# One load per head for V, wo ahead of the values, and a four-group closing in a cached decode-attention kernel

## The chip, the cores and the metric

The kernel runs on one core of a Trainium2 chip. TensorE multiplies, VectorE and ScalarE do elementwise work and reductions, GpSimd does small elementwise work, and SyncE (SP) issues the transfers; 16 DMA engines carry them out. The metric is the device time of one execution, in microseconds. Before the change it is 220.58 us, the median of three runs (220.52 to 221.18).

## The reference

One decode step of two batch rows, `x` of 2 x 512. Everything is float32.

```python
W = 4096                                     # the last 4096 of 32768 cached positions
q = (x @ wq)                                 # 32 query heads of 128; 8 KV heads, 4 queries share one
scores = einsum("bhqd,bhkd->bhqk", q, k) * 128 ** -0.5
p = softmax(scores)
a = einsum("bhqk,bhkd->bhqd", p, v).reshape(B, 1, 32 * 128) @ wo     # 4096 x 512
h = einsum("bsd,df->bsf", x, w1) + b1        # 512 x 1792
b = einsum("bsf,fd->bsd", h * tanh(softplus(h)), w2)                 # 1792 x 512
g = sigmoid((x * gate_w).sum(-1))
return g * a + (1 - g) * b
```

K and V in the window are 33.5 MB each; wq and wo 8.4 MB each; w1 and w2 3.7 MB each. Each of these bytes is used once.

## The kernel before, in words

The work is a loop of eight rounds, one for each KV head, on every engine. Buffers are single: `kslot` holds one head's K (128 x 8192) and the next head's slice of wq (128 x 2048); `vslot` holds V (128 x 8192, named `vs`), a slice of w2 (`w2s`, 128 x 1024) and a slice of wo (`wos`, 128 x 2048). w1 is resident in `w1s`. The last slice of wo has its own place, `wol`.

A round goes so. When K has landed, TensorE makes the scores `sc` (line 233: 16 products in four column groups of 32), while VectorE makes the next head's queries (line 325) and then copies them into `qz` (line 288). VectorE takes the maximum `mx` (line 329), TensorE transposes it into `mb` (line 239), VectorE makes the bias (line 333), ScalarE the exponentials (line 214), TensorE their sums `lp` (line 240), VectorE transposes the probabilities to `pT` (line 335). TensorE then multiplies them with V into `o` (line 244: 16 products of 128x512, again four column groups; products 0 to 7 use the first half of V). Of `o` (128 x 512) only one 128-column block in each row group is wanted. VectorE picks it with four masked multiply-adds into `osc` (lines 342 and 344; `mkr` is mask, gate and one over the sum). TensorE folds the row groups with one product into `ol` (line 257, tile `small`), and VectorE copies it to `wst2` (line 347). The MLP's hidden units go the same way once a round: VectorE multiplies w1 with x and sums (lines 336, 292, 298), GpSimd and ScalarE apply Mish, and the result goes to `hst`. With two products of w2 (line 253) and four of wo (line 260) the round adds both into the PSUM tile `acc`. These use the attention output and hidden units of the round before, so the slices of w2 and wo that come with V belong to the head before.

SP issues all transfers in program order, and each waits for its buffer to be free: K of the next head for `qz` (VectorE has used both the scores' operands and wq), the first half of V for `sV` (TensorE is through products 0 to 7 of `o`), the rest with w2 and wo for `sP` (the round's last product of wo is done). In the last round K comes in three pieces, V in three (`va`, `v7b`, `v7c`), then w2 (`w26`), wo of head 6 (`wo6`) and wo of head 7 in three pieces (`wo7a`, `wo7b`, `wo7c`).

After the loop ScalarE copies `acc` to `accs` (line 218), and TensorE folds it and multiplies the last slice of wo in the function `last`: each call makes two products of 256 columns in two column groups, with two row halves of `fin` for two sets of calls. ScalarE copies one half (line 220), VectorE adds the other (line 351), and SP stores `res`.

Of the kernel before, what the change touches and what calls it, by code (L numbers as in the profile page):

```python
# [36 lines left out]
def decode_kernel(nc, xg, wq0, w1, kw, k7a, k7b, k7c, va, vb0, vb, v7b, v7c, w26, wo6, wo7a, wo7b, wo7c, out):  # L37
# [78 lines left out]
    for i in range(HKV):  # L116
# [7 lines left out]
        if i:  # L124
            SP.wait_ge(sem["sV"], i)
        SP.dma_start(vs[:, : 2 * h], va[i]).then_inc(sem["ld_v"], L)
        if i:
            SP.wait_ge(sem["sP"], i)
        if i == 0:
            SP.dma_start(vs[:, 2 * h :], vb0).then_inc(sem["ld_vb"], L)  # L130
            SP.dma_start(w1s[:, : PAIRS * W1P], w1).then_inc(sem["ld_w"], L)
        elif i < PAIRS:
            SP.dma_start(vslot[:, 2 * h : CHUNK + 2 * D + WQH], vb[i - 1]).then_inc(sem["ld_vb"], L)
        else:
            SP.dma_start(vs[:, 2 * h : 3 * h], v7b).then_inc(sem["ld_vb"], L)
# [76 lines left out]
    with A.Fori(1, HKV + 1, 1) as r:
# [3 lines left out]
        A.activation(pq, pq, AF.Exp).then_inc(sem["hq"], 1)  # L216
# [1 line left out]
    A.copy(accs, acc).then_inc(sem["accs"], 1)
# [1 line left out]
    A.copy(fs, fin[64:, :256]).then_inc(sem["fs"], 1)  # L220


    key_rhs = same[:, :16].rearrange("p (b n h) -> p b n h", b=B, n=NH)[:, :, 0, :]
    with T.Fori(1, HKV + 1, 1) as r:
# [27 lines left out]
        for j in range(2):
            i = T.matmul(acc[Q * j : Q * j + Q, :], hst[:, j * Q : j * Q + Q], w2s[:, j * D : j * D + D],  # L253
                         start=False, stop=False, skip_group_check=True)
# [2 lines left out]
        after(T.matmul(ol, osel, key_rhs, start=True, stop=True), "osel").then_inc(sem["sE"], 1)  # L257
        T.wait_ge(sem["ld_o"], loads)
        for j in range(REP):
            i = T.matmul(acc[Q * j : Q * j + Q, :], wst[:, j * Q : j * Q + Q], wos[:, j * D : j * D + D],  # L260
                         start=False, stop=False, skip_group_check=True)
        i.then_inc(sem["sP"], 1)

    def last(s, lhs, rhs, wait=None, **kw):
        for u in range(2):
# [1 line left out]
            i = T.matmul(fin[a : a + Q, :256], lhs, rhs[:, u * 256 : u * 256 + 256], skip_group_check=True, **kw)  # L267
# [137 lines left out]
```

## Time and profile before

| | us |
|---|---|
| median of three runs | 220.58 |
| profiled execution, its own time | 220.1 |
| its span, first to last instruction | 218.8 |
| TensorE busy | 118.8 (54%) |
| VectorE busy | 126.2 (58%) |
| ScalarE busy | 10.3 (5%) |
| GpSimd busy | 26.2 (12%) |
| DMA queue q1, share of 16 engines' span | 97.8% |

Busy shares are averages over the span. "PE" is TensorE's matmuls, "PEld" its weight loads, "DVE" VectorE, "ACT" ScalarE, "POOL" GpSimd, "SPq" the queue of SP. A float32 product appears as two matmul records and two weight loads. "PEclk" is the clock that TensorE was granted: 1.00 is full, 0.50 half. A row of a timeline can merge several like instructions that follow each other; its count stands behind the x, and the square bracket tells how long the engine had been idle before, and what ended that.

### The profile page before, as it was taken

How to read it: one execution, taken by the hardware profiler on the slowest of the kernel's cores; microseconds unless marked ns; L12 is line 12 of the kernel's file. 1: busy time of each engine (PE TensorE's matmuls, PEld its weight loads, DVE VectorE, ACT ScalarE, POOL GpSimd, SP SyncE). 2: the span in 40 equal slices, each digit the busy share in tenths (PEclk: the TensorE clock that was granted, in tenths of full speed). 3: DMA queues.
4: the chain of work that ended last, by engine and by line, in shares of the span. 5: the costliest groups of instructions: out<-in, count | busy, mean ns of one | idle time of the engine just before them, and what ended most of it. 6: DMA issues, size and time to landing. Idle time of an engine off the chain costs nothing.

```text
span 218.8 us, 1985 instructions
## 1 busy us (share of the span) xinstructions
PE 118.8 (54%) x668; PEld 31.1 (14%) x668; DVE 126.2 (58%) x268; ACT 10.3 (5%) x28; POOL 26.2 (12%) x118
## 2 busy tenths in 40 slices
PE   0006386058463477807547195924648175984775
PEld 0002021012110112202111022101112022120211
DVE  2897913919743468507673177714693075967850
ACT  2000010000100001000100001000100001000101
POOL 8200000220021000310012000210002100050030
PEclk9999958757969675875988757695996958599599
DMA  8898999989999999989999899999999899999993
GB/s 310 367 479 371 453 446 407 479 377 429 451 434 442 401 437 455 464 374 452 435 407 479 377 429 446 439 442 401 437 455 464 374 446 440 392 412 442 412 410 118
DMA packets 4926, 91.29 MB, mean 417 GB/s; under 512 B 552, under 2 KB 572, under 8 KB 1084
## 3 DMA queue, kind: packets, MB, share of 16 engines
q1 hardware_dynamic: 4924, 91.26, 97.8%
q8 instruction: 1, 0.02, 0.0%
q14 instruction: 1, 0.01, 0.0%
HBM read 91.26 MB, written 0.00 MB: 417 GB/s over the span
## 4 chain that ended last, share of the span: by engine, by line
DMA 73%; PE 15%; DVE 8%; SPq 2%; issue 1%; DVEq 0%
DMA vslot<-in_vb 51%; DMA w1s<-in_w 15%; PE o L244 9%; DMA wol<-in_wo7a 8%; PE acc L260 4%; DVE osc L344 3%; PE small L257 1%; DVE osc L342 1%; DVE junk L292 1%; DVE hxt L298 1%; PE fin L267 1%; SPq L113 0%; DVE w1c L336 0%; DVE xs L300 0%; SPq L137 0%
## 5 line engine op out<-in xcount | busy, mean ns | idle before, releaser
L233 PE MATMUL sc<-kslot,zeros 128*32 128x512 f32 x256 | 42.7, 823 | 51.5 <-DMA kslot<-in_kw 50.2
L325 DVE CUSTOM_DVE_ANT_0 junk<-kslot,xs 128x512 f32<-128x512 f32 x64 | 39.8, 686 | 37.4 <-DMA kslot<-in_kw 36.4
L244 PE MATMUL o<-vslot,pT 128*32 128x512 f32 x256 | 48.2, 897 | 12.8 <-DMA vslot<-in_vb 10.1
L233 PEld LDWEIGHTS sc<-kslot,zeros 128*32 128x32 f32 x256 | 10.7, 145 | 83.2 <-issue 80.4
L187 POOL TENSOR_TENSOR hb<-hxt,zeros 128x4 f32<-128x4 f32 x8 | 1.7, 216 | 147.0 <-DVE hxt L298 147.0
L292 DVE TENSOR_TENSOR junk<-w1c,xs 128x2048 f32<-128x2048 f32 x8 | 18.3, 2293 | 0.3
L298 DVE TENSOR_REDUCE hxt<-junk 128x4 f32<-128x2048 f32 x8 | 18.3, 2286 | 0.3
L244 PEld LDWEIGHTS o<-vslot,pT 128*32 128x32 f32 x256 | 9.2, 147 | 42.4 <-issue 19.1
L342 DVE TENSOR_SCALAR osc<-o,mkr 128x128 f32<-128x128 f32 x8 | 2.8, 351 | 15.1 <-PE o L244 15.1
L214 ACT ACTIVATE prob<-sc,bias 128x512 f32<-128x512 f32 x8 | 5.5, 687 | 118.7 <-DVE bias L333 118.7
L257 PE MATMUL small<-same,osc 128*128 128x8 f32 x16 | 3.3, 280 | 12.7 <-DVE osc L344 12.7
L240 PE MATMUL small<-lsum,same 128*128 128x1 f32 x16 | 4.1, 324 | 10.5 <-ACT prob L214 10.5
L260 PE MATMUL acc<-vslot,zeros 128*32 128x512 f32 x64 | 9.4, 662 | 0.6 <-DMA vslot<-in_wo 0.6
L335 DVE STREAM_TRANSPOSE pT<-prob 128x512 f32<-128x512 f32 x8 | 5.7, 712 | 6.8 <-ACT prob L214 6.8
L336 DVE COPY w1c<-w1s 128x1024 f32 x8 | 5.2, 656 | 7.5 <-DMA w1s<-in_w 7.5
L344 DVE SCALAR_TENSOR_TENSOR osc<-o,mkr,osc 128x128 f32<-128x128 f32 x24 | 8.4, 351 | 0.9
L253 PE MATMUL acc<-vslot,zeros 128*32 128x512 f32 x32 | 8.6, 616 | 0.3 <-DMA vslot<-in_w 0.3
L329 DVE TENSOR_REDUCE mx<-sc 128x1 f32<-128x512 f32 x8 | 5.5, 691 | 5.6 <-PE sc L233 5.6
L239 PE MATMUL mb<-ident,mx 128*128 128x128 f32 x8 | 2.6, 322 | 9.1 <-DVE mx L329 9.1
L257 PEld LDWEIGHTS small<-same,osc 128*128 128x128 f32 x16 | 2.6, 203 | 20.2 <-DVE osc L344 20.2
L325 DVE DVE_READ_ACCUMULATOR2_ANT q<- 128x1 f32 x64 | 5.2, 81 | 0.0
L240 PEld LDWEIGHTS small<-lsum,same 128*128 128x128 f32 x16 | 3.4, 265 | 12.0 <-ACT prob L214 12.0
(63 smaller groups left out, 64.8 us busy)
## 6 DMA issues: line engine op xcount, KB each, us to landing
kslot<-in_kw SPq DMA_DIRECT2D x7, 5120.0 KB, 19.3
vslot<-in_vb SPq DMA_DIRECT2D x6, 3584.0 KB, 18.9
vslot<-in_va SPq DMA_DIRECT2D x8, 2048.0 KB, 19.9
w1s<-in_w SPq DMA_DIRECT2D x1, 3584.0 KB, 32.7
vslot<-in_vb SPq DMA_DIRECT2D x1, 2048.0 KB, 24.6
kslot<-in_k7a SPq DMA_DIRECT2D x1, 2048.0 KB, 11.1
vslot<-in_wq SPq DMA_DIRECT2D x1, 1031.0 KB, 5.2
kslot<-in_k7b SPq DMA_DIRECT2D x1, 1024.0 KB, 13.2
```

The costliest lines, as they stand in the source:

```text
L214: A.activation(prob, sc, AF.Exp, bias=bias, scale=SCALE, accum_out=lsum).then_inc(sem["ex"], 1)
L233: i = T.matmul(sc[Q * j : Q * j + Q, :], qz[:, m * Q : m * Q + Q], ks[:, (m * NJ + j) * 512 : (m * NJ + j + 1) * 512], start=(m == 0), sto ...
L240: after(T.matmul(lp, same, lsum, start=True, stop=True), "ex").then_inc(sem["sC"], 1)
L244: i = T.matmul(o[Q * j : Q * j + Q, :], pT[:, c * Q : c * Q + Q], vs[:, c * 512 : c * 512 + 512], start=(c < NJ), stop=(c >= NC - NJ))
L253: i = T.matmul(acc[Q * j : Q * j + Q, :], hst[:, j * Q : j * Q + Q], w2s[:, j * D : j * D + D], start=False, stop=False, skip_group_check= ...
L257: after(T.matmul(ol, osel, key_rhs, start=True, stop=True), "osel").then_inc(sem["sE"], 1)
L260: i = T.matmul(acc[Q * j : Q * j + Q, :], wst[:, j * Q : j * Q + Q], wos[:, j * D : j * D + D], start=False, stop=False, skip_group_check= ...
L292: return V.tensor_tensor(out.rearrange("p (b c d) -> p b c d", b=B, c=n), lhs.rearrange("p (c d) -> p c d", c=n)[:, None, :, :].to_broadca ...
L298: return V.tensor_reduce(out, junk[:, : n * D].rearrange("p (c d) -> p c d", d=D), axis=AX.X, op=ALU.add)
L325: i = V.tensor_tensor_reduce(out=junk[:, (h * B + b) * D : (h * B + b) * D + D], in0=wqs[:, h * D : h * D + D], in1=xb[b], op0=ALU.mult, o ...
L335: after(V.transpose(pT, prob), "ex").then_inc(sem["pT"], 1)
L344: after(V.scalar_tensor_tensor(osc[:, m * DH : m * DH + DH], o[:, m * DH : m * DH + DH], mkr[:, m : m + 1], osc[:, m * DH - DH : m * DH], ...
```

## The change

It is one edit of many parts.

- **V in one load.** For the heads 1 to 6, one transfer (`vw`) brings wo, V and w2; head 0 brings V in one. It is issued when `sP` comes. `sV` is gone. In the last round the first piece (`v7a`) holds wo of head 6 and the first half of V, so that `wo6` is no transfer of its own, and lies ahead of `v7b`, `v7c` and `w26` in the queue. The bias b1 moves to the front of `vslot`, padded to 16 columns.
- **wo ahead of the values.** On TensorE the four products of wo stand ahead of those of `o`, and `sP` is raised by the w2 products.
- **Output copied by ScalarE in halves.** ScalarE copies `o` to `osb` in two pieces of 256 columns. VectorE's four masked steps are gone.
- **Masked in small products.** `kmr` (128 x 32: mask, gate, one over the sum and row-group key) is made by VectorE right after the transpose of the probabilities, from the constant `m4gk` that GpSimd makes once. Four small products of `osb` with slices of `kmr` accumulate into `ol`, behind the raising of `sP`.
- **Closing in four column groups.** `last` makes four products of 128 columns, one in each column group; there are five calls, fold first. VectorE copies `fin` to `res` (128 x 128) alone.
- **Loop at a block boundary.** An alignment instruction stands ahead of TensorE's loop.

```diff
-        if i:
-            SP.wait_ge(sem["sV"], i)
-        SP.dma_start(vs[:, : 2 * h], va[i]).then_inc(sem["ld_v"], L)
-        if i:
-            SP.wait_ge(sem["sP"], i)
         if i == 0:
-            SP.dma_start(vs[:, 2 * h :], vb0).then_inc(sem["ld_vb"], L)
+            SP.dma_start(vs, v0).then_inc(sem["ld_v"], L)
             SP.dma_start(w1s[:, : PAIRS * W1P], w1).then_inc(sem["ld_w"], L)
-        elif i < PAIRS:
-            SP.dma_start(vslot[:, 2 * h : CHUNK + 2 * D + WQH], vb[i - 1]).then_inc(sem["ld_vb"], L)
+            continue
+        SP.wait_ge(sem["sP"], i)
+        if i < PAIRS:
+            SP.dma_start(row, vw[i - 1]).then_inc(sem["ld_v"], L)
         else:
+            SP.dma_start(row[:, : WQH + 2 * h], v7a).then_inc(sem["ld_v"], L)
             SP.dma_start(vs[:, 2 * h : 3 * h], v7b).then_inc(sem["ld_vb"], L)
             SP.dma_start(vs[:, 3 * h :], v7c).then_inc(sem["ld_vc"], L)
             SP.dma_start(w2s, w26).then_inc(sem["ld_h"], L)
-    SP.dma_start(wos, wo6).then_inc(sem["ld_o"], L)
...
+        A.wait_ge(sem["sD"], r)
+        for m in range(2):
+            A.copy(osb[:, m * 2 * DH : m * 2 * DH + 2 * DH], o[:, m * 2 * DH : m * 2 * DH + 2 * DH]).then_inc(sem[f"os{m + 1}"], 1)
     A.wait_ge(sem["sP"], HKV)
     A.copy(accs, acc).then_inc(sem["accs"], 1)
-    A.wait_ge(sem["pe"], 1)
-    A.copy(fs, fin[64:, :256]).then_inc(sem["fs"], 1)
...
+    T.addr_align(256, offset=0, max_nops=0)
     with T.Fori(1, HKV + 1, 1) as r:
...
         T.wait_ge(sem["ld_v"], loads)
+        for j in range(REP):
+            i = T.matmul(acc[Q * j : Q * j + Q, :], wst[:, j * Q : j * Q + Q], wos[:, j * D : j * D + D],
+                         start=False, stop=False, skip_group_check=True)
+            if j == 0:
+                after(i, "hs")
         for c in range(NC):
             j = c % NJ
             i = T.matmul(o[Q * j : Q * j + Q, :], pT[:, c * Q : c * Q + Q], vs[:, c * 512 : c * 512 + 512],
                          start=(c < NJ), stop=(c >= NC - NJ))
             if j == 0 and c != NJ:
                 after(i, ("pT", "", "ld_vb", "ld_vc")[c // NJ])
-            if c == NC // 2 - 1:
-                i.then_inc(sem["sV"], 1)
         i.then_inc(sem["sD"], 1)
         T.wait_ge(sem["ld_h"], loads)
         for j in range(2):
             i = T.matmul(acc[Q * j : Q * j + Q, :], hst[:, j * Q : j * Q + Q], w2s[:, j * D : j * D + D],
                          start=False, stop=False, skip_group_check=True)
             if j == 0:
-                after(i, "hs")
-        after(T.matmul(ol, osel, key_rhs, start=True, stop=True), "osel").then_inc(sem["sE"], 1)
-        T.wait_ge(sem["ld_o"], loads)
-        for j in range(REP):
-            i = T.matmul(acc[Q * j : Q * j + Q, :], wst[:, j * Q : j * Q + Q], wos[:, j * D : j * D + D],
-                         start=False, stop=False, skip_group_check=True)
+                after(i, "kmr")
         i.then_inc(sem["sP"], 1)
-
-    def last(s, lhs, rhs, wait=None, **kw):
-        for u in range(2):
-            a = Q * (2 * s + u)
-            i = T.matmul(fin[a : a + Q, :256], lhs, rhs[:, u * 256 : u * 256 + 256], skip_group_check=True, **kw)
-            if wait is not None and u == 0:
+        for m in range(BN):
+            i = T.matmul(ol, osb[:, m * DH : m * DH + DH], kmr[:, m * B * REP : (m + 1) * B * REP],
+                         start=(m == 0), stop=(m == BN - 1))
+            if m % 2 == 0:
+                after(i, f"os{m // 2 + 1}")
+        i.then_inc(sem["sE"], 1)
+
+    def last(lhs, rhs, wait, **kw):
+        for u in range(NJ):
+            i = T.matmul(fin[Q * u : Q * u + Q, :P], lhs, rhs[:, u * P : u * P + P], skip_group_check=True, **kw)
+            if u == 0:
                 i.wait_op(*wait, "sem-ge")
         return i
 
-    def wo(j):
-        return wst2[:, j * Q : j * Q + Q], wol[:, j * D : j * D + D]
-
+    last(fold, accs, (sem["accs"], 1), start=True, stop=False)
     T.wait_ge(sem["wst"], HKV)
-    last(0, *wo(0), (sem["ld_w0"], L), start=True, stop=False)
-    last(1, *wo(1), start=True, stop=False)
-    last(0, fold, accs, (sem["accs"], 1), start=False, stop=False)
-    last(1, *wo(2), (sem["ld_w1"], L), start=False, stop=True).then_inc(sem["pe"], 1)
-    last(0, *wo(3), (sem["ld_w2"], L), start=False, stop=True).then_inc(sem["pe"], 1)
+    for j, (n, value) in enumerate((("ld_w0", L), ("wst", HKV), ("ld_w1", L), ("ld_w2", L))):
+        i = last(wst2[:, j * Q : j * Q + Q], wol[:, j * D : j * D + D], (sem[n], value), start=False, stop=(j == REP - 1))
+    i.then_inc(sem["pe"], 1)
...
+        after(V.reciprocal(rcp, lp), "sC").then_inc(sem["rcp"], 1)
+        after(V.tensor_scalar_mul(kmr, m4gk, rcp), "rcp").then_inc(sem["kmr"], 1)
         at(V.tensor_copy(w1c, w1s[:, bass.ds((r - 1) * W1P, W1P)]), "ld_w", 2 * L).then_inc(sem["w1c"], 1)
         after(products(junk[:, : 2 * B * D], w1c, 2), "w1c").then_inc(sem["w1p"], 1)
         after(sums(hxt, 2 * B), "w1p").then_inc(sem["hx"], 1)
-        after(V.reciprocal(rcp, lp), "sC").then_inc(sem["rcp"], 1)
-        after(V.tensor_scalar_mul(mkr, m4g, rcp), "rcp").then_inc(sem["mkr"], 1)
-        V.wait_ge(sem["sD"], r)
-        after(V.tensor_scalar_mul(osc[:, :DH], o[:, :DH], mkr[:, 0:1]), "mkr").then_inc(sem["os1"], 1)
-        for m in range(1, BN):
-            after(V.scalar_tensor_tensor(osc[:, m * DH : m * DH + DH], o[:, m * DH : m * DH + DH], mkr[:, m : m + 1],
-                                         osc[:, m * DH - DH : m * DH], op0=ALU.mult, op1=ALU.add),
-                  f"os{m}").then_inc(sem["osel" if m == BN - 1 else f"os{m + 1}"], 1)
         after(V.tensor_copy(wst2v, ol.rearrange("p (b h) -> p h b", b=B)), "sE").then_inc(sem["wst"], 1)
         after(V.reciprocal(mr, md), "hd").then_inc(sem["hr"], 1)
     V.addr_align(128, offset=0, max_nops=0)
-    V.wait_ge(sem["fs"], 1)
-    at(V.tensor_tensor(res, fin[:64, :256], fs, op=ALU.add), "pe", 2).then_inc(sem["res"], 1)
+    at(V.tensor_copy(res, fin[:, :P]), "pe", 1).then_inc(sem["res"], 1)
...
-        "va": v[:, :, : 2 * h],
-        "vb0": v[0, :, 2 * h :],
-        "vb": np.concatenate([v[1:PAIRS, :, 2 * h :], w2[:NP], wo[:NP]], axis=2),
+        "v0": v[0],
+        "vw": np.concatenate([wo[: NP], v[1:PAIRS], w2[:NP]], axis=2),
+        "v7a": np.concatenate([wo[NP], v[PAIRS, :, : 2 * h]], axis=1),
         "v7b": v[PAIRS, :, 2 * h : 3 * h], "v7c": v[PAIRS, :, 3 * h :],
-        "w26": w2[NP], "wo6": wo[NP],
+        "w26": w2[NP],
```

On SP, from the load of head 6's K to the end, the transfers stood in this order before (`kw` is K with wq; `va`, `vb`, `v7b`, `v7c` are pieces of V; `w` is the last w2, `wo` the slice of head 6):

```order
L120 DMA kslot<-in_kw 128x10240
L126 DMA vslot<-in_va 128x4096
L133 DMA vslot<-in_vb 128x7168
L123 DMA kslot<-in_k7a 128x4096
L123 DMA kslot<-in_k7b 128x2048
L123 DMA kslot<-in_k7c 128x2048
L126 DMA vslot<-in_va 128x4096
L135 DMA vslot<-in_v7b 128x2048
L136 DMA vslot<-in_v7c 128x2048
L137 DMA vslot<-in_w 128x1024
L138 DMA vslot<-in_wo 128x2048
```

And now:

```order
L119 DMA kslot<-in_kw 128x10240
L129 DMA vslot<-in_vw 128x11264
L122 DMA kslot<-in_k7a 128x4096
L122 DMA kslot<-in_k7b 128x2048
L122 DMA kslot<-in_k7c 128x2048
L131 DMA vslot<-in_v7a 128x6144
L132 DMA vslot<-in_v7b 128x2048
L133 DMA vslot<-in_v7c 128x2048
L134 DMA vslot<-in_w 128x1024
```

Two rows became one for each of the heads 1 to 6, and the row of `wo` went up into `v7a`; the three pieces of `wo7` follow in both.

On TensorE, in the loop and behind it (- before, + now; `mb` and `small` are the maximum's transpose and the sums, `o` the values, `acc` the products of w2 and wo, `fin` the closing):

```order
 L239 MATMUL mb<-ident,mx 128x128
 L240 MATMUL small<-lsum,same 128x1
-L244 MATMUL o<-vslot,pT 32x512 x16
-L253 MATMUL acc<-vslot,zeros 32x512 x2
-L257 MATMUL small<-same,osc 128x8
-L260 MATMUL acc<-vslot,zeros 32x512 x4
+L243 MATMUL acc<-vslot,zeros 32x512 x4
+L249 MATMUL o<-vslot,pT 32x512 x16
+L256 MATMUL acc<-vslot,zeros 32x512 x2
+L262 MATMUL small<-kmr,osb 128x8 x4
```

The four products of wo moved from the round's end to a place ahead of the values, and the fold into `ol` (tile `small`) is four products at the end of the round.

More of the change, by code (lines that the diff above doesn't have):

```diff
@@ L34, with decode_kernel @@
 NP = PAIRS - 1
-def decode_kernel(nc, xg, wq0, w1, kw, k7a, k7b, k7c, va, vb0, vb, v7b, v7c, w26, wo6, wo7a, wo7b, wo7c, out):
+def decode_kernel(nc, xg, wq0, w1, kw, k7a, k7b, k7c, v0, vw, v7a, v7b, v7c, w26, wo7a, wo7b, wo7c, out):
     T, V, A, G, SP = nc.tensor, nc.vector, nc.scalar, nc.gpsimd, nc.sync
@@ L49, in decode_kernel @@
     w1c = sb("w1c", W1P)
-    vslot = sb("vslot", CHUNK + 2 * D + WQH + 2 * HKV)
-    vs, w2s, wos = vslot[:, :CHUNK], vslot[:, CHUNK : CHUNK + 2 * D], vslot[:, CHUNK + 2 * D : CHUNK + 2 * D + WQH]
-    b1 = vslot[:, CHUNK + 2 * D + WQH : CHUNK + 2 * D + WQH + FC]
+    vslot = sb("vslot", Q // B + WQH + CHUNK + 2 * D)
+    b1, row = vslot[:, :FC], vslot[:, Q // B :]
+    wos, vs, w2s = row[:, :WQH], row[:, WQH : WQH + CHUNK], row[:, WQH + CHUNK :]
     wol = sb("wol", REP * D)
@@ L80, in decode_kernel @@
     rcp = sb("rcp", 1)
-    mkr = sb("mkr", BN)
-    osc = sb("osc", BN * DH)
-    osel = osc[:, (BN - 1) * DH :]
+    m4gk = sb("m4gk", BN * B * REP)
+    kmr = sb("kmr", BN * B * REP)
+    osb = sb("osb", BN * DH)
     junk = sb("junk", B * REP * D)
@@ L93, in decode_kernel @@
     accs = sb("accs", D)
-    fs = sb("fs", 256, 64)
-    res = sb("res", 256, 64)
+    res = sb("res", P)
     acc = ps("acc", D)
@@ L104, in decode_kernel @@
     ol = small[:, 8:16]
-    names = ("ld_x ld_q ld_k ld_kb ld_kc ld_v ld_vb ld_vc ld_w ld_h ld_o ld_w0 ld_w1 ld_w2 c_id c_m c_z c_xb c_eg c_g c_mg "
-             "gx g0 g1 g2 g3 g4 g5 hs vx q8 rcp os1 os2 os3 qz mx sA sB bias ex pT sC osel sD sP sE sV wst pq mkr w1c w1p hx hq hd hr accs pe fs res st").split()
+    names = ("ld_x ld_q ld_k ld_kb ld_kc ld_v ld_vb ld_vc ld_w ld_h ld_w0 ld_w1 ld_w2 c_id c_m c_z c_xb c_eg c_g c_mg "
+             "gx g0 g1 g2 g3 g4 g5 hs vx q8 rcp os1 os2 qz mx sA sB bias ex pT sC sD sP sE wst pq kmr w1c w1p hx hq hd hr accs pe res st").split()
     sem = {n: nc.alloc_semaphore(n) for n in names}
-    SP.dma_start(vslot[:, CHUNK + 2 * D : CHUNK + 2 * D + WQH + FC], wq0).then_inc(sem["ld_q"], L)
+    SP.dma_start(vslot[:, : Q // B + WQH], wq0).then_inc(sem["ld_q"], L)
     SP.wait_ge(sem["c_xb"], 2)
@@ L174, in decode_kernel @@
     G.wait_ge(sem["c_g"], 1)
-    G.tensor_tensor(m4g.rearrange("p (b n) -> p b n", n=NH), m2[:, :BN].rearrange("p (b n) -> p b n", n=NH),
-                    g[:, :, None].to_broadcast([P, B, NH]), op=ALU.mult)
-    G.tensor_scalar(omg, g, -1.0, 1.0, op0=ALU.mult, op1=ALU.add).then_inc(sem["c_mg"], 1)
+    done(G.tensor_tensor(m4g.rearrange("p (b n) -> p b n", n=NH), m2[:, :BN].rearrange("p (b n) -> p b n", n=NH),
+                    g[:, :, None].to_broadcast([P, B, NH]), op=ALU.mult))
+    G.tensor_scalar(omg, g, -1.0, 1.0, op0=ALU.mult, op1=ALU.add)
+    G.tensor_tensor(m4gk.rearrange("p (m b h) -> p m b h", b=B, h=REP),
+                    same[:, :16].rearrange("p (b n h) -> p b n h", b=B, n=NH)[:, :, 0, :][:, None].to_broadcast([P, BN, B, REP]),
+                    m4g[:, :, None, None].to_broadcast([P, BN, B, REP]), op=ALU.mult).then_inc(sem["c_mg"], 1)
     G.wait_ge(sem["c_mg"], 1)
@@ L205, in decode_kernel @@
                         omg[:, None, :].to_broadcast([P, 2, B]), op=ALU.mult).then_inc(sem["hs"], 1)
-    for n in ("ld_kb", "ld_kc", "ld_vc", "ld_o", "ld_h"):
+    for n in ("ld_kb", "ld_kc", "ld_vb", "ld_vc", "ld_h"):
         A.sem_inc(sem[n], AHEAD)
@@ L349, in decode_kernel @@
     V.addr_align(128, offset=0, max_nops=0)
-    V.wait_ge(sem["fs"], 1)
-    at(V.tensor_tensor(res, fin[:64, :256], fs, op=ALU.add), "pe", 2).then_inc(sem["res"], 1)
+    at(V.tensor_copy(res, fin[:, :P]), "pe", 1).then_inc(sem["res"], 1)
     SP.wait_ge(sem["res"], 1)
-    SP.dma_start(out, res[:: Q // B, :]).then_inc(sem["st"], L)
+    SP.dma_start(out.rearrange("b u x -> u b x"), res[:: Q // B, :]).then_inc(sem["st"], L)
     SP.wait_ge(sem["hs"], HKV + 1)
@@ L399 @@
             for n, t in arrays.items()]
[L400 removed]
+    args.append(nc.dram_tensor("out_0", (B, NJ, P), F32, kind="ExternalOutput").ap())
     decode_kernel(nc, *args)
     r = run_bass_kernel_spmd(nc, [{f"in_{n}": t for n, t in arrays.items()}], core_ids=[0])
[L403 to L404 removed]
+    y = r.results[0]["out_0"]
+    return c(y).reshape(B, 1, D)
```

6 lines of the change are left out of this document (1 added, 5 removed).

## The prediction

> **What bounds the kernel now.** I began with the page's DMA part and the table of busy time by stretches, because a kernel that uses each byte once may have nothing left but its transfers.
>
> ```profile
> span 218.8 us, 1985 instructions
> ...
> q1 hardware_dynamic: 4924, 91.26, 97.8%
> q8 instruction: 1, 0.02, 0.0%
> ```
>
> ```profile
> 2.00:50.00 48.00, 16.98 (x89) 4.71 (x93) 29.07 (x47) 1.54 (x5) 7.17 (x28) 0.84 0.99 425
> ...
> 150.00:200.00 50.00, 32.69 (x194) 8.57 (x194) 32.67 (x79) 1.97 (x6) 5.90 (x24) 0.79 1.01 430
> 200.00:213.00 13.00, 8.84 (x49) 2.39 (x41) 8.99 (x18) 0.99 (x3) 1.71 (x9) 0.74 1.00 414
> 213.00:216.00 3.00, 2.60 (x26) 0.75 (x28) 0.00 (x0) 0.79 (x2) 0.67 (x4) 1.00 0.69 255
> 216.00:218.80 2.80, 0.41 (x4) 0.00 (x0) 0.42 (x1) 0.16 (x1) 0.00 (x0) 1.00 0.01 1
> ```
>
> The columns behind the length are the busy time of PE, PEld, DVE, ACT and POOL, then the granted clock, the DMA share and GB/s. The DMA share is 0.99 to 1.01 from 2 us to 213 us: the 16 engines never run dry, and no compute inside the loop sets the time, though the chain of waits passes through it. Only three things can move the end: how long the transfers take, whether the queue runs dry, and what follows the last landings. The span ends 218.8 us and the execution counts 220.1, so 1.3 us lie outside it.
>
> So I read the end next, from the timeline.
>
> ```profile
> 204.49 5.95 PE L244 MATMUL o<-vslot,pT 128*32 128x512 f32 x32 [0.90 <-DMA vslot<-in_va]
> ...
> 209.38 0.16 PEld L244 LDWEIGHTS o<-vslot,pT 128*32 128x32 f32 x8 [1.27 <-DMA vslot<-in_v7c]
> ...
> 209.99 0.21 ACT L216 ACTIVATE pq<-pq 128x8 f32<-128x8 f32 x1 [7.04 <-POOL pq L191]
> ...
> 210.73 1.05 PE L253 MATMUL acc<-vslot,zeros 128*32 128x512 f32 x4 [0.29 <-DMA vslot<-in_w]
> ...
> 212.15 0.30 PEld L257 LDWEIGHTS small<-same,osc 128*128 128x128 f32 x2 [1.27 <-DVE osc L344]
> 212.15 0.39 PE L257 MATMUL small<-same,osc 128*128 128x8 f32 x2 [0.36 <-DVE osc L344]
> 212.57 0.17 DVE L347 COPY wst<-small 128x8 f32<-128x8 f32 x1 [0.48 <-PE small L257]
> ...
> 213.15 0.16 PEld L260 LDWEIGHTS acc<-vslot,zeros 128*32 128x32 f32 x8 [0.70 <-DMA vslot<-in_wo]
> ...
> 214.28 0.59 ACT L218 COPY accs<-acc 128x512 f32<-128x512 f32 x1 [4.08 <-PE acc L260]
> ...
> 214.43 0.16 PEld L267 LDWEIGHTS fin<-wol,wst 128*32 128x32 f32 x8 [1.12 <-DMA wol<-in_wo7a]
> ...
> 215.36 1.05 PE L267 MATMUL fin<-wol,wst 128*32 128x256 f32 x6
> 215.78 0.14 PEld L267 LDWEIGHTS fin<-wol,wst 128*32 128x32 f32 x4 [0.52 <-DMA wol<-in_wo7c]
> 215.79 0.37 ACT L220 COPY fs<-fin 64x256 f32<-64x256 f32 x1 [0.93 <-PE fin L267]
> 216.46 0.42 DVE L351 TENSOR_TENSOR res<-fin,fs 64x256 f32<-64x256 f32 x1 [3.63 <-PE fin L267]
> ```
>
> Each product that starts on a landing tells when that landing came: the first half of V 204.49, v7c 209.38, w26 about 210.7, wo6 213.15, wo7a 214.43, wo7c 215.78. Behind the last one stand 0.63 us of products (to 216.41), 0.42 us of VectorE and the store. Everything between v7c and wo7c had 6.4 us of transfers to hide under.
>
> **The transfers.** Eight transfers vanish: one for each of heads 0 to 6, and wo6. The bytes stay. The price of a transfer's boundary comes from the same rows: 1,024 KB took 2.45 us (wo6, 210.70 to 213.15); 512 KB took 1.32 (w26) and 1.28 (wo7a); twice 256 KB took 1.35 (wo7b and c). Two halves cost 0.15 more than the whole, two quarters 0.03 to 0.07 more than a half. I take 0.08 for each, nearer the smaller ends because the rows give 0.01 us and handovers blur the rest: 8 x 0.08 = 0.64 us, with 0.2 and 1.2 as ends. That moves every landing near the end forward.
>
> [...]
>
> **Does the queue run dry?** V is now reloaded in one piece after the whole round, where its first half used to go out early. The shortest cover is head 7's K.
>
> ```profile
> 189.63 2.91 PE L244 MATMUL o<-vslot,pT 128*32 128x512 f32 x16 [0.32 <-DMA vslot<-in_vb]
> ...
> 195.70 0.33 SPq L135 DMA_DIRECT2D vslot<-in_v7b  x1
> ...
> 199.49 0.16 PEld L233 LDWEIGHTS sc<-kslot,zeros 128*32 128x32 f32 x8 [2.19 <-DMA kslot<-in_k7c]
> ```
>
> From head 6's V landing (189.63) to K's end (199.49) lie 9.9 us. TensorE then has six steps of four products: wo, four of values, and w2 (two products, but two passes all the same). A step's length depends on the granted clock.
>
> ```profile
> 186.53 0.20 PEld L244 LDWEIGHTS o<-vslot,pT 128*32 128x32 f32 x4 [0.66 <-issue]
> ...
> 187.38 0.20 PEld L244 LDWEIGHTS o<-vslot,pT 128*32 128x32 f32 x4 [0.66 <-issue]
> ...
> 195.46 0.13 PEld L233 LDWEIGHTS sc<-kslot,zeros 128*32 128x32 f32 x4 [0.30 <-issue]
> 195.89 0.13 PEld L233 LDWEIGHTS sc<-kslot,zeros 128*32 128x32 f32 x4 [0.30 <-issue]
> ```
>
> ```profile
> 48.60:51.73 3.13, 3.06 (x16) 0.92 (x20) 3.13 (x11) 0.00 (x0) 0.00 (x0) 0.50 1.01 429
> ...
> 184.85:191.68 6.83, 6.28 (x30) 1.69 (x34) 6.17 (x6) 0.02 (x1) 0.47 (x3) 0.50 0.93 398
> ...
> 201.92:208.74 6.82, 4.83 (x23) 1.63 (x26) 5.91 (x6) 0.78 (x2) 0.00 (x0) 0.50 0.97 404
> 208.74:218.70 9.96, 6.14 (x50) 1.37 (x42) 2.56 (x10) 1.16 (x3) 2.38 (x12) 1.00 0.65 256
> ```
>
> Four loads are two products: 0.85 us at clock 0.50, 0.43 at 1.00. A step is 1.70 cold and 0.86 warm. A burst after a pause starts cold and warms after 3.1 us (48.60 row), 4.25 (204.49 to 208.74), or as much as 6.8 (184.85 row). Call that x; n steps take x + (n - x/1.70) x 0.86. [...]
>
> Six steps take 7.3 us at x = 4.25 and 8.5 at 6.8. The issue takes 0.33, and a store took 1.1 us from its issue's end to landing, which bounds the delay to first data:
>
> ```profile
> SPq L357 <- DMA out<-res: 1.1, 1, 1.1
> ```
>
> That makes 8.7 to 9.95 us against 9.9. So I cost the late reload at nothing; in earlier rounds K is 5,120 KB instead of 4,096 KB and the cover longer still. On SP only the next K waits behind it, and that needs the scores of a K not yet landed.
>
> **The end, worked out.** wo now precedes v7a's values, so this landing comes at 204.49 + 2.45 - 0.64 = 206.30. TensorE's five steps (wo, sixteen values) end, with the same burst's x = 4.25, at 4.25 + 2.5 x 0.86 = 6.40, so 212.70. v7c (209.38 + 2.45 - 0.64 = 211.19) and w26 (212.51) have landed by then. w2: 0.86, to 213.56; `sP` rises and ScalarE's `accs` (0.59) hides under what follows. ScalarE's two copies of `o` were started at 212.7; at 0.37 each (64x256 row; 128x512 took 0.59) they are done by 213.6, and their place behind the exponential of `pq` costs nothing, because that ran at 209.99. Four small products: two loads in 0.30 each and a drain of 0.09: 1.29, to 214.85. Their copy on VectorE with handovers (212.54 to 212.77): 0.23, to 215.08. The fold ran meanwhile. A closing call of four 128-column products is a quarter of a warm step, 0.215: three of them to 215.72. The last: 0.215 plus the drain seen before (0.63 less two passes of 0.215) 0.20, to 216.14. Before it was 216.41: 0.27 saved.
>
> Then VectorE copies 128x128 from PSUM. This exact form is not in the trace; it lies between 0.17 (128x8) and 0.35 (`osc`, same size, multiply):
>
> ```profile
> L342 DVE TENSOR_SCALAR osc<-o,mkr 128x128 f32<-128x128 f32 x8 | 2.8, 351 | 15.1 <-PE o L244 15.1
> ```
>
> I take 0.30 for 0.42: 0.12 saved. ScalarE's half (0.37) overlapped TensorE and frees nothing. The sum is 0.27 + 0.12 = 0.39: 220.1 becomes 219.7. The median of the runs is 0.48 above the profiled execution, so **220.2 us**.
>
> The point is that the end changes its owner: 0.64 us of earlier landings and a shorter close are mostly eaten by TensorE's longer path after v7a, since 1 MB that used to lie behind the values now lies ahead of them. The last landing, 215.14, would allow 215.14 + 0.42 = 215.56.
>
> At nothing I cost: the four removed VectorE steps, about 1.5 us a round, since the reload has the cover above; `kmr` ahead of w1 (it needs two small operations beside products on TensorE); `m4gk`, one GpSimd operation before the first round, under head 0's loads; and the alignment, executed while TensorE waits for the first K. That the branch back cost a code load each round is not seen: queue q8 shows one packet in the span.
>
> The ends: with x = 3.1 the values end at 212.13 and w26's landing decides: 212.51 + 0.86 + 1.29 + 0.23 + 0.64 + 0.42 = 215.95, 220.0 in all. With x = 6.8 they end at 213.96 and the products at 217.40: 0.99 - 0.12 = 0.87 later, 221.45. The ends of the transfers' price shift this by +0.4 and -0.6.
>
> **Rivals.** *A, faster: the close hides again.* If the small products overlap (their weight loads can run under the w2 products) and warm clock comes early, the last landing decides: 215.56, so 0.85 + 0.12 = 0.97 saved, 219.6; with 1.2 us from the transfers 219.1. For it: weight loads overlap matmuls in the rows above, and a better x. Against: the 0.30 us for two loads is what TensorE takes even with nothing beside it.
>
> *B, slower: the values run cold.* With the values crowded behind v7a, x over 6.5 puts the end 0.7 us or more back: 221.3 to 221.45. For it: 6.83 us cold in the 184.85 row. Against: two of the three rows are shorter. Before, this could not be seen, since wo6 and wo7 covered it. It decides from x = 6.5 on.
>
> *C, slower: the queue runs dry before v7a*, from x = 6.8 on or a longer first-data delay than 1.1 us: each us of delay adds one us, and every landing behind it slides; at 1 us more 221.2 or above.
>
> [...]
>
> **Chances.** Forecast 0.47, A 0.34, B 0.11, C 0.05, D 0.03. Faster by over 0.3% (below 219.9, about what this kernel's measurement can tell from no change) is A and D: 0.37. Within 0.3%: 0.47. Slower (above 221.2): 0.16. The range, 219.3 to 221.3, takes in most of A and reaches B's beginning; the forecast's own is 219.9 to 221.2.
>
> **What would show it.** The DMA share stays at 1.00 up to about 215 us, with the last landing 0.2 to 1.2 earlier; a gap before v7a shows C. The last products begin on TensorE's own work or `wst` rather than on wo7c; if they begin on wo7c, A holds. The four small products should take 1.3 us. The clock in the rows from v7a on gives x. I am wrong if the transfers slow down with the longer rows, or if the last landing moves by more than 1.2 us.

## The result, and the profile after

The changed kernel takes 223.12 us, the median of six runs (221.45 to 224.31). The kernel before, run beside it, takes 220.50 (220.11 to 221.18). The ratio is 1.012, with a 95% interval of 1.0092 to 1.0147: it is 1.2% slower. The prediction was 220.2, with a range of 219.3 to 221.3. The profiled execution of the changed kernel took 222.79.

From its page come the span, two of the queues, and the chain that ended last:

```profile
span 221.5 us, 2089 instructions
...
q1 hardware_dynamic: 3776, 91.26, 96.9%
q8 instruction: 2, 0.03, 0.1%
...
DMA 69%; PE 28%; issue 1%; SPq 0%; DVE 0%
```

The bytes are the same, in 1,148 packets fewer. Queue q8, of the kind "instruction", has one packet more; its packets are called code loads here. Busy time by stretches, with the columns as before:

```profile
2.00:50.00 48.00, 14.66 (x88) 5.44 (x89) 26.32 (x39) 2.07 (x7) 7.38 (x29) 0.86 1.01 431
...
150.00:200.00 50.00, 29.73 (x174) 9.67 (x174) 24.78 (x54) 3.27 (x10) 4.33 (x23) 0.73 0.98 420
200.00:213.00 13.00, 8.46 (x58) 2.84 (x61) 11.16 (x28) 0.78 (x2) 1.91 (x4) 0.76 0.99 400
213.00:216.00 3.00, 3.00 (x26) 0.90 (x20) 1.29 (x1) 0.21 (x2) 0.93 (x5) 0.88 0.99 401
```

DMA still moves 401 GB/s from 213 to 216 us, where it had fallen to 255 before: everything lands later. How much later, and since when, TensorE's timeline tells, whose products start on the landings. First the kernel before, then the changed one:

```profile
18.24 4.99 PE L233 MATMUL sc<-kslot,zeros 128*32 128x512 f32 x32 [18.24 <-DMA kslot<-in_kw]
...
48.67 5.13 PE L233 MATMUL sc<-kslot,zeros 128*32 128x512 f32 x32 [2.49 <-DMA kslot<-in_kw]
...
99.73 5.21 PE L233 MATMUL sc<-kslot,zeros 128*32 128x512 f32 x32 [6.34 <-DMA kslot<-in_kw]
```

```profile
19.65 5.05 PE L233 MATMUL sc<-kslot,zeros 128*32 128x512 f32 x32 [19.65 <-DMA kslot<-in_kw]
...
49.99 5.24 PE L233 MATMUL sc<-kslot,zeros 128*32 128x512 f32 x32 [3.43 <-DMA kslot<-in_kw]
...
100.91 5.34 PE L233 MATMUL sc<-kslot,zeros 128*32 128x512 f32 x32 [3.10 <-DMA kslot<-in_kw]
...
191.26 1.93 PE L243 MATMUL acc<-vslot,zeros 128*32 128x512 f32 x8 [4.18 <-DMA vslot<-in_vw]
...
199.28 0.33 SPq L131 DMA_DIRECT2D vslot<-in_v7a  x1
...
209.25 1.93 PE L243 MATMUL acc<-vslot,zeros 128*32 128x512 f32 x8 [0.69 <-DMA vslot<-in_v7a]
210.93 5.00 PE L249 MATMUL o<-vslot,pT 128*32 128x512 f32 x32
215.75 1.04 PE L256 MATMUL acc<-vslot,zeros 128*32 128x512 f32 x4
216.71 1.06 PE L262 MATMUL small<-kmr,osb 128*128 128x8 f32 x8
...
218.13 1.08 PE L270 MATMUL fin<-wol,wst 128*32 128x128 f32 x32
219.26 0.29 DVE L343 COPY res<-fin 128x128 f32<-128x128 f32 x1 [1.21 <-PE fin L270]
```

The first K already lands 1.41 us late (19.65 against 18.24), before any part of the loop has run. Up to 100.91 the delay shrinks to 1.18: the merged loads do save. Then it grows, to 1.63 at head 6's V (191.26 against the 189.63 of before), and the first half of head 7's V lands at 209.25, 2.9 us after the 206.30 of the prediction. It was issued at 199.28, and that was too late: in the transfer records (start, duration and size of every DMA packet) the first engines run out of head 7's K at about 199.0, at 200.1 only 5 of the 16 carry a packet, and the first packet of V starts at 200.24. This is the gap before `v7a` that the prediction named as the sign of rival C. From the landing to the end the close goes as worked out: the last product ends about 10.0 us after it, where 9.84 were predicted.

### The profile page after: what moved, and what is told of

It is laid out like the page before. It is cut to its first block, busy times and chain, and to the rows that moved or that the text cites. A ratio compares the mean times of both kernels' runs of the same rounds, so it can differ in the third digit from the quotient of the medians.

```text
span 221.5 us, 2089 instructions
## 1 busy us (share of the span) xinstructions
PE 119.0 (54%) x736; PEld 40.6 (18%) x736; DVE 115.0 (52%) x236; ACT 15.0 (7%) x43; POOL 26.1 (12%) x119
## 4 chain that ended last, share of the span: by engine, by line
DMA 69%; PE 28%; issue 1%; SPq 0%; DVE 0%
DMA vslot<-in_vw 53%; PE o L249 17%; DMA vslot<-in_v 12%; PE acc L243 7%; DMA vslot<-in_v7a 4%; PE acc L256 3%; PE fin L270 1%; PE small L262 0%; SPq L112 0%; DVE xs L299 0%; SPq L119 0%; DVE res L343 0%
## 5 line engine op out<-in xcount | busy, mean ns | idle before, releaser
L249 PE MATMUL o<-vslot,pT 128*32 128x512 f32 x256 | 39.4, 767 | 0.0
L243 PE MATMUL acc<-vslot,zeros 128*32 128x512 f32 x64 | 15.5, 1056 | 30.2 <-DMA vslot<-in_vw 28.9
L340 DVE COPY wst<-small 128x8 f32<-128x8 f32 x8 | 1.4, 172 | 52.3 <-PE small L262 52.3
L249 PEld LDWEIGHTS o<-vslot,pT 128*32 128x32 f32 x256 | 12.0, 147 | 32.0 <-issue 32.0
L262 PE MATMUL small<-kmr,osb 128*128 128x8 f32 x64 | 9.3, 272 | 8.3 <-ACT osb L218 8.3
L262 PEld LDWEIGHTS small<-kmr,osb 128*128 128x128 f32 x64 | 8.6, 208 | 15.1 <-ACT osb L218 15.1
L256 PE MATMUL acc<-vslot,zeros 128*32 128x512 f32 x32 | 8.3, 592 | 0.0
L243 PEld LDWEIGHTS acc<-vslot,zeros 128*32 128x32 f32 x64 | 1.8, 140 | 30.7 <-issue 30.7
L218 ACT COPY osb<-o 128x256 f32<-128x256 f32 x16 | 5.2, 374 | 27.3 <-PE o L249 27.3
L215 ACT ACTIVATE pq<-pq 128x8 f32<-128x8 f32 x8 | 1.7, 208 | 67.6 <-POOL pq L190 67.6
```

The source lines that it names most:

```text
L249: i = T.matmul(o[Q * j : Q * j + Q, :], pT[:, c * Q : c * Q + Q], vs[:, c * 512 : c * 512 + 512], start=(c < NJ), stop=(c >= NC - NJ))
L262: i = T.matmul(ol, osb[:, m * DH : m * DH + DH], kmr[:, m * B * REP : (m + 1) * B * REP], start=(m == 0), stop=(m == BN - 1))
```

## The experiments

First, the delay that is there before the loop. `e1` takes out one line, the alignment ahead of TensorE's loop:

```diff
-    T.addr_align(256, offset=0, max_nops=0)
```

> The changed kernel without the alignment instruction ahead of TensorE's loop. In the changed kernel a code load of 2.06 us appears at 1.9 us, the first load lands 1.4 us later (6.6 us after its issue instead of 5.2) and head 0's K lands at 19.65 instead of 18.24. Theory 1 (the alignment makes TensorE load code at the start, and the one DMA engine that carries it stays behind, so every landing is late): head 0's K lands at about 18.3 again, and since the end hangs on the landing of v7a, the time falls by about 1.3 us, to 221.5 to 222.0. Theory 2 (the late reload of V alone is the cause): K lands later for another reason, and the time stays within 0.4 us of 223.1. Theory 3 (the cold close alone): within 0.5 us of 223.1 as well.

`e2` puts the same line into the kernel before.

> The kernel before, with the alignment instruction ahead of TensorE's loop and nothing else. Theory 1: head 0's K lands at about 19.6, all later landings about 1.4 us later, and 221.6 to 222.0 us in all. Theory 2 and 3: 220.5, no change.

Measured: `e1` 221.50 us, ratio 1.0049 (1.0031 to 1.0067); `e2` 220.87, ratio 1.0028 (1.0017 to 1.0039). The first K lands at 18.21 without the alignment and at 19.03 with it. One row of each, `e1` first:

```profile
18.21 6.03 PE L232 MATMUL sc<-kslot,zeros 128*32 128x512 f32 x32 [18.21 <-DMA kslot<-in_kw]
```

```profile
19.03 6.33 PE L234 MATMUL sc<-kslot,zeros 128*32 128x512 f32 x32 [19.03 <-DMA kslot<-in_kw]
```

The transfer records show what the aligned kernels do there, and a like event later in a kernel without the alignment (`e5`, below). These are the code loads (packets on q8) ahead of the close:

```
kernel       start us   took us   KB
after          1.91      2.06     16
e2             2.25      0.97     16
e3             2.32      1.27     16
e5            38.72      0.99     16
all others     none
```

While one of the 16 engines does this, its share of the data waits, and it stays behind. The lag, from the moment the first engine goes on to the next load to the end of the slowest engine's last packet, tells how far. For the very first load (wq) it is 2.25 us in the changed kernel, 1.7 in `e3` and 1.37 in `e2`; in the fourteen traces without a code load there it is 0.20 to 0.93. From the first K to the first piece of head 7's K it is 1.5 to 2.5 in the changed kernel, about 1.1 in `e2` and 0.4 to 0.5 in the kernel before. At `v7a` in the changed kernel, where the queue pauses, the lag shrinks from 1.56 to 0.56. TensorE began only when the slowest engine was through: the first K's sixteen completion marks in the changed kernel's trace run from 17.71 to 19.52 us, and the first product starts at 19.65; in the kernel before they run from 17.66 to 18.10, and it starts at 18.24. So the alignment costs about 1.6 us in the changed kernel (223.12 less 221.50) and 0.5 to 0.6 in the kernel before. `e2` fell short of its expectation of 221.6 to 222.0: its code load took half as long, and its first K was 0.79 us late instead of 1.41. One trace of each does not show why the loads differ.

Next, the dry queue: the engines without work ahead of `v7a`. `e3` issues head 7's first half of V when half of head 6's values are done, as before; `e4` does so without the alignment too.

```diff
+            SP.wait_ge(sem["sV"], i)
             SP.dma_start(row[:, : WQH + 2 * h], v7a).then_inc(sem["ld_v"], L)
+            SP.wait_ge(sem["sP"], i)
```

> The changed kernel, but head 7's first V piece with wo is issued when TensorE is through the first half of head 6's values, not after the whole round. Theory 2 (the queue runs dry before v7a, since it is issued at 199.28 and head 7's K has left the engines by 199.9 to 200.5): the gap at 199 to 201 us closes, v7a lands 0.7 to 1.3 us earlier after head 7's K, and 221.8 to 222.5 us. Theory 1 alone: 223.1, since the lag of the one engine stays. Theory 3: 223.1.

> Both edits: no alignment, and the early issue of v7a. If both theories hold, the gains add: about 2 us, 220.8 to 221.4, and what is left over 220.5 is the close, in which TensorE is 1.8 us behind the last landing. If theory 1 alone holds, as without the alignment; if theory 2 alone, as with the early issue.

Measured: `e3` 222.92 (ratio 1.0137, 1.0091 to 1.0182), no better than the change; its code load took 1.27 us at 2.32, and other V loads had slow packets, so it tells nothing alone. `e4` has 221.19, ratio 1.0018 (0.9994 to 1.0042), with runs from 219.84 to 221.85. Beside `e1` the early issue is worth about 0.7 us by the ratios, whose intervals overlap, and 0.3 by the medians.

Part of what `e4` loses comes after its last instruction. Its profiled execution took 221.54 us with a span of 219.50, so that 2.04 lie outside the span, and its one code load runs from 220.85 to 221.78, behind the span's end. The same holds for `e5b` below (2.04 outside, code load from 220.23 to 221.15, span 218.88). In the fifteen other traces no code load stands behind the span's end, and 1.32 to 1.43 us lie outside. Of the runs, four of ten of `e4`, three of ten of `e5b`, two of ten of `e1` and two of four of `e3` have 1.9 to 2.6 us outside; every other run of any kernel here has 1.5 or less. By the spans alone, the medians are 219.9 for `e1`, 219.15 for `e4` and 219.0 for the kernel before: the early issue is worth about 0.75 us, and little is left inside the span. What puts that code load so late in some executions stays open. The spans of `e4` still spread by 2.2 us (218.3 to 220.5), those of the kernel before by 1.0.

Is it the clock behind that landing? `e5` and `e5b` add idle products, whose result nothing reads, to `e4`: four and two in a round.

> The kernel with both edits (no alignment, early v7a), and four idle products of 128x512 a round on TensorE whose result nobody uses: two behind the scores, one behind the maximum's transpose, one ahead of the wait for V. They keep TensorE busy up to v7a's landing. Theory A (the close hangs on the clock: the values start cold at v7a, and the time to full clock, 3.1 to 6.8 us, sets the end and scatters from run to run; with both edits the runs go from 219.8 to 221.9): full clock at v7a, the values end about 1 us earlier, median 220.0 to 220.5, and the runs lie within about 1 us. Theory B (the place of wo ahead of the values is enough to hold the close, clock or not): median within 0.3 us of 221.2, spread as before. If the idle products themselves delay the path: above 221.5.

> The changed kernel without alignment and with head 7's first half of V issued early, and two idle products a round (one behind the scores, one ahead of the wait for V, into a tile that nothing reads) that keep TensorE's clock up. Theory (the loss left in that kernel, some 0.7 us, and the spread of its runs by 2 us, are the clock at which the sixteen values behind the first half of V run): granted clock 1.00 from the first half of V on or within 2 us of it, 220.2 to 220.8 with runs within 1 us. Rival (the loss is the order itself, wo's megabyte ahead of the values): about 221.2 even with a full clock. If a code load of 16 KB shows up within the loop's first round, the run tells neither.

Measured: `e5` 222.27 (1.0093), confounded by the code load above. `e5b` 221.26 (1.0053, 1.0023 to 1.0083) with runs from 220.07 to 223.20. In the profiled executions the granted clock from 205 to 214 us is 0.81 in `e5b` against 0.62 in `e4`, yet neither the median nor the spread came down. This speaks against the clock there, but does not rule it out: the clock of `e5b` was 0.50 up to 209.63, 2.7 us behind the landing, and full clock was expected within 2 us.

Then the parts at the other end. `e6` is the kernel before with the new closing alone; `e7` adds ScalarE's copies and the small masked products, with loads and wo as before.

> The kernel before with the new closing alone: four products of 128 columns a call in four column groups, one copy of 128x128 by VectorE, no ScalarE half. In the kernel before 0.63 us of products and 0.42 us of VectorE follow the last landing; the changed kernel's rows show 0.29 us for the copy, and 128 columns should need 0.42 us. Expected by the prediction's step: 0.3 to 0.35 us saved, 220.0 to 220.1. If the close is bound elsewhere: 220.4, no change.

> Everything of the change that moves no load: the new closing, ScalarE's copies of the output, the small masked products. V comes in two loads with wo behind the values as before, no alignment. If the loss of the change sits in the loads, in wo's place and in the alignment alone: as the closing alone, 219.9 to 220.2. If ScalarE's copies and the four small products (1.0 us of weight loads a round against 0.3 before) cost too: 220.4 or more, with TensorE's part of the close starting later than the last landing.

Measured: `e6` 220.13, ratio 0.9991 (0.9981 to 1.0000); `e7` 220.31, 0.9996 (0.9984 to 1.0007). None of these costs anything that the measurement shows, and neither gains clearly. That leaves the alignment and the moved loads.

`e8` keeps V in one load for heads 0 to 6, but leaves wo behind the values and wo of head 6 in a load of its own.

> V in one load for heads 0 to 6 (issued when the round's last product of wo is done), head 7's first half of V issued early as before, wo behind the values and wo of head 6 as a transfer of its own behind w26; the new closing, ScalarE's copies and the small products; no alignment. Theory (the loss left after alignment and the early first half are taken care of comes from wo ahead of the values, which lengthens TensorE's path behind the last large landing): the seven merges are worth 7 x 0.08 = 0.56 us and the close is hidden again, so 219.6 to 219.9, and runs lie within 0.8 us of each other. Rival (the single late load of V costs in every round by itself): 220.5 or more. Last products begin on wo7c by the theory.

Measured: 220.96, ratio 1.0028 (1.0013 to 1.0042), as the rival forecast. With wo behind the values there is still a loss, and it lies inside the span (median span 219.65 against 218.9 before). The late single load is common to `e4` and `e8`; why `e8` loses more inside the span than `e4` stays open. Yet `e8`'s profiled execution took 219.77, and a second one 220.39:

> The kernel with merged V and wo behind the values (median 220.96, its profiled run 219.77), looked at again. If it takes 220.7 or more, lead-time theory: some V load is issued less than 3 us ahead and shows slow first packets there; rivals as for e10: an engine late from the first K on, a code load, a cold close.

Both are among the faster executions, and the first shows the merges at their worth. From `e8`'s profiled execution, K and V of heads 1, 5 and 6:

```profile
18.17 5.36 PE L234 MATMUL sc<-kslot,zeros 128*32 128x512 f32 x32 [18.17 <-DMA kslot<-in_kw]
48.51 5.54 PE L234 MATMUL sc<-kslot,zeros 128*32 128x512 f32 x32 [3.44 <-DMA kslot<-in_kw]
61.83 5.71 PE L245 MATMUL o<-vslot,pT 128*32 128x512 f32 x32 [4.96 <-DMA vslot<-in_vw]
...
150.31 5.84 PE L234 MATMUL sc<-kslot,zeros 128*32 128x512 f32 x32 [4.34 <-DMA kslot<-in_kw]
163.64 6.00 PE L245 MATMUL o<-vslot,pT 128*32 128x512 f32 x32 [4.66 <-DMA vslot<-in_vw]
175.75 5.07 PE L234 MATMUL sc<-kslot,zeros 128*32 128x512 f32 x32 [3.41 <-DMA kslot<-in_kw]
189.07 5.24 PE L245 MATMUL o<-vslot,pT 128*32 128x512 f32 x32 [5.43 <-DMA vslot<-in_vw]
```

From the first K to head 6's V are 170.90 us, against 171.39 before: seven merges, 0.07 us each. And each of these V lands 13.3 us after its K.

To test the late issue itself, `e11` makes it later by about 1.3 us, and changes nothing else:

```diff
-            SP.wait_ge(sem["sP"], i)
+            SP.wait_ge(sem["sE"], i)
             SP.dma_start(vslot[:, : CHUNK + 2 * D + WQH], vw[i - 1]).then_inc(sem["ld_v"], L)
```

> The kernel with merged V and wo behind the values (220.96 median), its V load issued later on purpose: it waits for the small products behind the last product of wo, about 1.3 us more; no other instruction changes. Theory (lead time): every lead falls from 3.3 to 4.4 us to 2.0 to 3.1 us, slow first packets at most of the five loads, 0.3 to 0.8 us lost in each on the slowest engine, median 222 or more. Rival (spread by something else; the cover of 12 us still hides the issue): 221.0, unchanged.

Measured: 225.87 us, ratio 1.025 (1.0218 to 1.0282), 4.9 us more than `e8`. The same rows, and the issue of head 5's V:

```profile
18.20 5.51 PE L234 MATMUL sc<-kslot,zeros 128*32 128x512 f32 x32 [18.20 <-DMA kslot<-in_kw]
48.54 5.69 PE L234 MATMUL sc<-kslot,zeros 128*32 128x512 f32 x32 [3.43 <-DMA kslot<-in_kw]
63.35 5.12 PE L245 MATMUL o<-vslot,pT 128*32 128x512 f32 x32 [6.28 <-DMA vslot<-in_vw]
...
152.70 6.52 PE L234 MATMUL sc<-kslot,zeros 128*32 128x512 f32 x32 [3.76 <-DMA kslot<-in_kw]
167.24 6.07 PE L245 MATMUL o<-vslot,pT 128*32 128x512 f32 x32 [5.20 <-DMA vslot<-in_vw]
179.36 5.14 PE L234 MATMUL sc<-kslot,zeros 128*32 128x512 f32 x32 [3.34 <-DMA kslot<-in_kw]
193.85 6.42 PE L245 MATMUL o<-vslot,pT 128*32 128x512 f32 x32 [6.52 <-DMA vslot<-in_vw]
```

```profile
148.97 0.33 SPq L128 DMA_DIRECT2D vslot<-in_vw  x1
```

V of heads 1, 5 and 6 now lands 14.81, 14.54 and 14.49 us after its K instead of 13.3, though the load of head 5 was issued 3.7 us before that K was seen to land. In `e8` the same load went out at 145.04, 5.3 us before. A load issued in what looked like good time still cost 1.2 us (14.54 against 13.3). The transfer records of the seventeen profiled executions show the pattern. The lead is the time from a load's issue to the moment the first engine reaches it; the extra is how much longer the load's slowest packet took than its middle one. The first two loads of each execution are left out: their leads are 1.0 and 2.3 to 2.7 us in every kernel, the kernel before included, and their extras 0.25 to 1.20.

```
lead, us      loads   extra of the slowest packet, us
under 2         13    0.74 to 1.69
2.0 to 3.1      20    0.01 to 1.67, 15 of them over 0.2
3.1 to 5.0      64    0.00 to 0.26, 2 of them over 0.2
over 5         375    0.00 to 0.50, 2 of them over 0.2
```

The 0.50 belongs to the K during whose transfer `e5` loaded code.

In the changed kernel the V loads of heads 2 to 5 have leads of 1.6 to 2.6 us and extras of 0.43 to 1.50, and head 7's first half a lead of 0.96 and an extra of 0.86. In the kernel before no V load has a lead under 6.

Two more kernels test the same from the other side. `e9` is `e7` with the first half of V issued together with the second:

```diff
-            SP.wait_ge(sem["sV"], i)
+            SP.wait_ge(sem["sV" if i == PAIRS else "sP"], i)
```

> Closing, ScalarE's copies and small products as changed, order of TensorE and number of transfers as before, no alignment; one thing added: in heads 1 to 6 the first half of V is issued together with the second, when the round's last product of wo is done, instead of after half the values. Theory: a V load that is issued less than about 3 us ahead of the moment at which the engines reach it costs the slowest engine 0.3 to 1.7 us, and these issues would stand 2.4 to 4.4 us ahead, some of them too late: median 220.8 to 221.2, runs spread over 2 us, slow first packets at the V loads with little lead. Rival (the long rows of the merged load cost, not the late issue): 220.3 with runs within 0.9 us, as with the early half.

Measured: 221.36, ratio 1.0043 (1.0029 to 1.0058), all runs within 0.6 us. The median lies just above the expected 220.8 to 221.2, and the way there was another. One load is late, head 1's:

```profile
47.78 0.33 SPq L125 DMA_DIRECT2D vslot<-in_va  x1
48.15 0.43 SPq L132 DMA_DIRECT2D vslot<-in_vb  x1
...
49.27 5.46 PE L235 MATMUL sc<-kslot,zeros 128*32 128x512 f32 x32 [1.55 <-DMA kslot<-in_kw]
```

It has a lead of 0.96 and an extra of 1.10. All its later V loads have leads over 4.6 and no extra. One dry spot early goes with a cost of 1 us (221.36 against the 220.31 of `e7`), without any merged load, and the runs of this kernel, whose other leads are long, don't spread.

`e10` is `e8` with the whole V issued as soon as its values are done, and w2 and wo in a load of their own.

> wo behind the values, whole V in one load as in the changed kernel, but issued as soon as the sixteen values are done, some 1.7 us earlier than with the products of w2 and wo behind them; w2 and wo come in a load of their own when those products are done. Theory (lead time): every V load now has 4.5 us of lead or more, no slow first packets there, 220.2 to 220.5 and runs within 1 us, though V is one load of 32 KB rows. Rival (the merged load itself): about 221 with 2 us of spread.

Measured: 221.65 (ratio 1.0042, 1.0019 to 1.0064), and not in one cluster: four runs from 220.17 to 220.56, five from 221.65 to 222.18. Its profiled run belongs to the first, with leads over 9 us and no extra. So the lead is not all. The same kernel ran twice more, for a trace of the slower group:

> The same kernel as with V issued behind the values (e10), looked at again. If this execution is of the slower group (221.7 to 222.2): by the lead-time theory nothing in the loop is slow (every lead is over 5 us but that of the first K, 2.5 us), so the 1.4 us must come from one engine that is held up at the first K's load and stays behind. Rivals: a code load of 16 KB inside the loop; a close that runs cold, with landings unchanged.

> As for the look before: a second chance of an execution of the slower group, with the same marks to tell a late engine from a code load and from a cold close.

They took 221.80 and 220.39. The first is the one wanted. Its V leads are over 8 us without extra, and there is no code load. Its end against that of the first profiled run, in stretches and in the timeline; first the 220.17 run:

```profile
215.50:218.20 2.70, 1.09 (x40) 0.82 (x32) 0.29 (x1) 0.00 (x0) 0.56 (x3) 0.92 0.03 9
```

```profile
212.88 1.06 PE L263 MATMUL acc<-vslot,zeros 128*32 128x512 f32 x8 [1.35 <-DMA vslot<-in_wo]
...
215.29 0.65 PE L276 MATMUL fin<-wol,wst 128*32 128x128 f32 x16 [0.35 <-DVE wst L350]
...
216.64 0.29 DVE L353 COPY res<-fin 128x128 f32<-128x128 f32 x1 [1.43 <-PE fin L276]
```

and the 221.80 run:

```profile
215.50:218.20 2.70, 2.36 (x40) 1.94 (x40) 0.21 (x3) 0.00 (x0) 0.76 (x4) 0.50 0.04 9
```

```profile
213.34 1.06 PE L263 MATMUL acc<-vslot,zeros 128*32 128x512 f32 x8 [1.35 <-DMA vslot<-in_wo]
...
215.75 1.08 PE L276 MATMUL fin<-wol,wst 128*32 128x128 f32 x16 [0.35 <-DVE wst L350]
...
218.17 0.29 DVE L353 COPY res<-fin 128x128 f32<-128x128 f32 x1 [2.49 <-PE fin L276]
```

The closing products run at clock 0.50 instead of 0.92: 2.42 us from their start to VectorE's copy instead of 1.35. That is 1.07 of the 1.63 us; 0.46 more came from later landings (213.34 against 212.88), and there the lag is 0.9 us from the first load on, against 0.2 to 0.4 in the 220.17 run. In this execution the clock at the close is the larger part of the difference; an engine that is late from the start, which the expectation named, is the smaller. Whether the other runs of that group and the slower runs of `e8` went the same way is not shown. None of these kernels beats the kernel before by more than can be measured.

## Why the prediction was wrong

- **The transfers' price was right.** 0.08 us a boundary was taken; `e8` shows 0.07.
- **"The alignment, executed while TensorE waits for the first K"** was costed at nothing. This step failed, with 1.6 us of the 2.6 by `e1`. TensorE indeed had time (its first product stood at 18.24 us before); a DMA engine had not. The price was looked for on the engine that executes the line, and it fell on the queue, which is the bound. The argument from one packet on q8 was about the branch back, and said nothing of a load at the start, which took 2.06 us.
- **"I cost the late reload at nothing"** failed too, and `e4` and `e11` show it. Two terms were wrong. The cover of 9.9 us ran from V's landing to K's landing as TensorE sees it. But the queue runs dry when the *first* engine has finished K: in the record of before that is about 198.5, not 199.49, so the cover was 8.9. And the delay to first data was bounded by a store's 1.1 us, with 0.33 for the issue, 1.4 together; the leads above ask for about 3.1. With x = 4.25 the need was 7.3 + 3.1 = 10.4, over the cover even in the good case. That puts rival C's mechanism into the forecast; its condition, x from 6.8 on, was wrong for the same reason. In the changed kernel the issue came 8.0 us after head 6's V, and the lag of the slow engine shortened the cover to about 7.7 (191.26 to 199.0).
- **"In earlier rounds the cover is longer still"** failed on the same 3.1 us: heads 2 to 5 had leads of 1.6 to 2.6 and lost some 0.7 us together (a delay of 1.63 less 1.41 at head 6's V, and the 0.49 that seven merges save).
- **v7a's landing at 206.30** came at 209.22, the start of the weight loads. Of the 2.9 us, 1.4 are the engine that the code load held up, some 0.7 the slow packets of heads 2 to 5, and the rest of some 0.8 arose at v7a itself and from merges worth a little less than taken. This is an account along one trace.
- **The close was right in mechanism.** x was 4.48 (4.25 taken), ScalarE's copies, the small products (1.06 against 1.29) and VectorE's copy (0.29 against 0.30) took what they should, and the last products began on TensorE's own work. Rival A did not occur, since the last products did not begin on wo7c; rival B's x of 6.5 didn't occur here; and no run shows the far larger saving by merged loads for which D's 0.03 stands: seven merges saved 0.5 us.
- **The range** held every unknown price but the two that were set to nothing. Neither had been given a bound.

## What to carry to other kernels

Where the DMA queue never pauses, count the cover of a reload from the record of the issue to the moment when the first DMA engine runs out, and leave over 3 us of it, by the table above (28 of 33 loads with a lead under 3.1 us had an extra over 0.2, and 4 of 439 with more lead); here, landing to landing flattered it by about 1 us. Count a code load as a transfer as well: here one of 2.06 us during the first load put the first K 1.41 us back and one of 0.97 put it 0.79 back, and in the changed kernel the delay was still 1.18 at 100.91 us. A move that saves eight boundaries of 0.07 us did not pay for one load issued late.

## What was not expected of the hardware

A code load of 16 KB took 0.97 to 2.06 us beside data transfers, while a data packet of 16,384 bytes took 0.61, and the engine that carried it stayed behind: where it ran during the first load, the lag there was 1.37 to 2.25 us, against 0.20 to 0.93 in the other traces. TensorE was waiting for its first K anyway, up to 18.24 us in the kernel before, and the cost fell on the queue. A lead of 2.0 to 3.1 us was not enough in 15 of 20 loads: their slowest packet took 0.2 to 1.67 us longer than the middle one. A code load behind the last instruction went with 0.6 to 0.7 us more outside the span (2.04 in `e4` and `e5b`, against 1.32 to 1.43). And the clock was 0.50 in the last microseconds of one execution of `e10` and 0.92 in those of another, with the same instructions; that was 1.07 of the 1.63 us between them.
